# A two-layer attention and MLP kernel: four block sums of a weight matrix made one turn later, and one of two squares made on ScalarE in all five passes

## The chip, the cores and the metric

The kernel runs on one core of a Trainium2 chip. The metric is the device time of one execution in microseconds (us). PE is the matmul engine, DVE is VectorE, ACT is ScalarE, POOL is GpSimd, SP is the queue that issues DMAs.

## The reference

Attention with a window of 128 positions over 4 x 8 heads of 576 positions, then two MLP layers on 2304 tokens of width 512 with a hidden width of 2048. Only the first layer's activation and the second layer's weights are touched by the change.

```python
attn_out = _attn_ref(q, k, v)                     # windowed softmax attention
x = attn_out.transpose(0, 2, 1, 3).reshape(B * S, H * D)     # 2304 x 512
# layer 1
h = x @ w_in                                      # 512 -> 2048
r = np.maximum(h, 0.0)
g = r * r
x = g @ w_out                                     # 2048 -> 512
# layer 2, with its own weights
h = x @ w_in2
y = (h * np.tanh(softplus(h))) @ w_out2
```

## The kernel before

All products are made in a reduced-precision matmul format, so that each operand is split into a high part (a rounded copy) and a low part (the operand less its high part), and three products stand for one.

**Passes and steps.** Layer 1 runs in five passes j = 0 to 4 over blocks of tokens, each with 16 steps fc, one for each 128 columns of the hidden layer. Step "2.8" below is pass 2, step 8. Pass 1 has 256 tokens and the others 512. In one step PE makes the scores of one attention unit of the next block, then `h` of this step (L594, 12 matmuls), at some steps transposes and attention outputs, and then the second product of the step before: `m_out` part 0 with the high part of `g` (L622, L623, 8 matmuls) and part 1 with the low part of `g` (L626, 4 matmuls). Every engine works through its own instructions in the order in which the code writes them.

**The activation of layer 1.** `relu2_a` makes r = relu(h) on ACT, the high part g[:,0] = r squared in the matmul format (ACT, L676), and gg = r squared in full fp32. In passes 0, 1 and 4 gg is made by ACT (L673), ahead of g; in passes 2 and 3 by POOL (L675). `relu2_b` makes the low part g[:,1] = gg - g[:,0] on DVE (L681), in the next step, ahead of that step's softmax. There is one tile r, one tile gg and two tiles g.

**The second layer's weights, prepared in passes 2 to 4.** A turn i (0 to 33) brings in one of 32 pieces of weights: ACT shifts it (`c_lower`, L843), DVE puts its bits together (`c_bits`, L848, L851, L854). Four pieces make a group m; turn 4m + r is its turn r. Pieces 4m and 4m + 1 belong to the first matrix, and the four sums of their blocks, `c_sums` (L866 to L869, tiles s), are made on DVE in passes 2 and 3 and on POOL in pass 4. The second matrix's sums (`c_sums2`, L880 to L884, tiles t) are always on POOL. Each finished tile is then split: ACT writes the high part (`c_split`, L892, tiles c), DVE puts the low part in place over the tile (`c_lows`, L935), and both are stored by DMA at the next step.

**Which steps have a turn.** Passes 2 and 3 have one at steps 2, 3, 4, 6, 7, 8, 10, 11, 12, 14, 15, eleven in each; pass 4 at steps 0 to 11. Turn 0 is at step 2.2, turn 11 at step 3.2, turn 22 at step 4.0. The order on DVE in a step with a turn is: low part of g of the step before (L681), softmax of a unit, bits of the turn's piece, sums if there are any, low parts of the tiles split in this turn. On POOL a step holds the low parts of the attention operands (L262, L264), the sums of the second matrix, gg in passes 2 and 3, and the masks of the probabilities (L473).

Of the kernel before, what the change touches and what calls it, by code (L numbers as in the profile page):

```python
# [13 lines left out]
AF = mybir.ActivationFunctionType  # L14
ALU = mybir.AluOpType
# [18 lines left out]
def two_layers(  # L34
# [16 lines left out]
    nc = tc.nc  # L51
# [91 lines left out]
    NB = len(blocks)  # L143
# [514 lines left out]
    def relu2_r(j, fc):  # L658
        n = size[j]
        ph = hps.pop((0, j, fc))  # L660
        r = gp.tile([P, 512], F32, tag="r", name=f"r{j}_{fc}")
        nc.scalar.activation(r[:, 0:n], ph[:, 0:n], AF.Relu)  # L662
        return r

    def relu2_a(j, fc, r=None):
        n = size[j]
        r = r or relu2_r(j, fc)
        g = gs[0, j, fc] = gp.tile([P, 2, 512], F32R, tag="g", name=f"g0_{j}_{fc}", bufs=2)
        gg = gp.tile([P, 512], F32, tag="gg", name=f"gg{j}_{fc}")
        if j in (0, 1, NB - 1):  # L670


            nc.scalar.activation(gg[:, 0:n], r[:, 0:n], AF.Square)  # L673
        else:
            nc.gpsimd.tensor_tensor(gg[:, 0:n], r[:, 0:n], r[:, 0:n], op=ALU.mult)  # L675
        nc.scalar.activation(g[:, 0, 0:n], r[:, 0:n], AF.Square)  # L676
        return g, gg, n

    def relu2_b(a):
# [149 lines left out]
    late, kept, wraw, wf = [], [], {}, {}  # L829
# [8 lines left out]
    def f_tile(name):  # L838
        return ap["c"].tile([P, DM], I32, tag="f", name=name, bufs=9)

    def c_lower(i):
        f = wf[i] = f_tile(f"wf1_{i}")
        nc.scalar.mul(f.bitcast(F32), wraw[i][:, :, 1].bitcast(F32), LOWERED)  # L843

    def c_bits(i):
        t, f = wraw.pop(i), wf[i]
        low, high = t[:, :, 0], t[:, :, 1]
        nc.vector.tensor_scalar(  # L848
            f, f, 3, 0x3FFFFFF8, op0=ALU.logical_shift_left, op1=ALU.bitwise_and
        )  # L850
        nc.vector.scalar_tensor_tensor(  # L851
            f, high, -0x40000000, f, op0=ALU.bitwise_and, op1=ALU.bitwise_or
        )
        nc.vector.scalar_tensor_tensor(  # L854
            f, low, 29, f, op0=ALU.logical_shift_right, op1=ALU.bitwise_or
        )
        wf[i] = f.bitcast(F32)

    def c_sums(m, eng):

        a, b = wf[4 * m], wf[4 * m + 1]
        x, y = (f_tile(f"s{m}_{k}").bitcast(F32) for k in range(2))
        wf["s", m] = x, y
        tt = eng.tensor_tensor
        s1, s2, s3, s4 = x[:, 0:256], x[:, 256:512], y[:, 0:256], y[:, 256:512]
        tt(s1, b[:, 0:256], b[:, 256:512], op=ALU.add)  # L866
        tt(s2, s1, a[:, 0:256], op=ALU.subtract)
        tt(s3, a[:, 0:256], b[:, 0:256], op=ALU.subtract)
        tt(s4, a[:, 256:512], s2, op=ALU.subtract)  # L869

    def c_sums2(m, half):

        b0, b1 = wf[4 * m + 2], wf[4 * m + 3]
        if half == 0:
            wf["t", m] = [f_tile(f"t{m}_{k}").bitcast(F32) for k in range(2)]
        x, y = wf["t", m]
        tt = nc.gpsimd.tensor_tensor
        t1, t2, t3, t4 = x[:, 0:256], x[:, 256:512], y[:, 0:256], y[:, 256:512]
        if half == 0:
            tt(t1, b0[:, 256:512], b0[:, 0:256], op=ALU.subtract)  # L880
            tt(t3, b1[:, 256:512], b0[:, 256:512], op=ALU.subtract)
        else:
            tt(t2, b1[:, 256:512], t1, op=ALU.subtract)
            tt(t4, t2, b1[:, 0:256], op=ALU.subtract)  # L884
# [4 lines left out]
    def c_split(f, dsts):  # L889
        n = f.shape[-1]  # L890
        hi = ap["c"].tile([P, DM], F32R, tag="c", name=f"c{len(wf)}", bufs=4)[:, 0:n]
        nc.scalar.copy(hi, f)  # L892
        late.append((f, hi, dsts))

    def in_w1d(m, at, n):
        return [w1d[m, :, at + k * n : at + (k + 1) * n] for k in range(2)]

    def in_t2d(m, k, many):
        dsts = [t2d[k : k + many, m, :, z * 256 : z * 256 + 256] for z in range(2)]
        return [d.rearrange("k p c -> p k c") for d in dsts]  # L900
# [11 lines left out]
    def c_tick1():  # L912

        m, r = divmod(made["at"], 4)
        if r == 0 and m:
            c_sums2(m - 1, 1)
            c_split(wf.pop(4 * m - 2)[:, 0:256], in_t2d(m - 1, 4, 1))
            c_split(wf.pop(4 * m - 1), in_t2d(m - 1, 5, 2))
        elif r == 1 and m:
            x, y = wf.pop(("t", m - 1))  # L920
            c_split(x, in_t2d(m - 1, 0, 2))
            c_split(y, in_t2d(m - 1, 2, 2))
        elif r == 2 and 4 * m < NW:
            c_split(wf.pop(4 * m), in_w1d(m, 0, 512))
            c_split(wf.pop(4 * m + 1)[:, 256:512], in_w1d(m, 1024, 256))
        elif r == 3 and 4 * m < NW:
            x, y = wf.pop(("s", m))
            c_split(x, in_w1d(m, 1536, 512))
            c_split(y, in_w1d(m, 2560, 512))
        if made["at"] < NW:  # L930
            c_lower(made["at"])

    def c_lows():
        for f, hi, dsts in late:
            nc.vector.tensor_tensor(f, f, hi.bitcast(F32), op=ALU.subtract)  # L935
            for dst, src in zip(dsts, (hi.bitcast(F32), f)):
                if len(dst.shape) == 3:
                    src = src.rearrange("p (d c) -> p d c", c=256)
                kept.append((dst, src))
        late.clear()  # L940

    def c_tick2(j):
        i = made["at"]
        made["at"] += 1
        m, r = divmod(i, 4)
        if i < NW:
            c_bits(i)
            if r == 1:
                c_sums(m, nc.vector if j < NB - 1 else nc.gpsimd)
            elif r == 3:  # L950
                c_sums2(m, 0)
        c_lows()
# [32 lines left out]
    for j in range(NB - 1):  # L985
        for fc in range(FC):
# [26 lines left out]
            if due:  # L1013
                c_tick1()
# [16 lines left out]
            if due:  # L1031
                c_tick2(j)
            m_h(0, j, fc, ps_h, "h")

            if last:
                for c in range(2):
                    x_split(j + 1, c, xp)
                r = relu2_r(j, fc)
            else:
                pend = relu2_a(j, fc)  # L1040
# [17 lines left out]
            if last:  # L1058
                for c in range(2, KC):
                    x_split(j + 1, c, xp)  # L1060
                pend = relu2_a(j, fc, r)
                for i in sc:
                    u_softmax1(i)
                    u_exp(i)
# [506 lines left out]
    j = NB - 1  # L1571
    for fc in range(FC):
# [6 lines left out]
        if due:  # L1579
            c_tick1()  # L1580
# [7 lines left out]
        if due:  # L1588
            c_tick2(j)
        m_h(0, j, fc, ps_h, "h")  # L1590
        pend = relu2_a(j, fc)
        m_out(*prev, 0)
        m_out(*prev, 1)
# [16 lines left out]
    for g in range(24):  # L1610
        s, m = divmod(g, 8)
# [159 lines left out]
```

## Time and profile before

| | |
|---|---|
| runs before | median 865.5 us of 3 (865.05 to 868.47) |
| the profiled execution | 864.87 us; its span 863.1 us, mean granted clock 0.998 |
| PE busy | 848.4 us, 98% |
| DVE, ACT, POOL busy | 654.1, 506.1 and 306.1 us |
| span by stage | pass 0 from about 37 us, pass 2 from about 200, pass 3 from about 305, pass 4 from about 413, the second layer from about 506 to the end |

The 1.8 us between the span and the execution's own time lie around the span. In a row of a timeline the first number is the start in us from the span's start and the second the busy time in us; "x4" means four instructions in one piece; a bracket at the end gives the idle time of that engine just before, and who ended it. Durations in rows on a tile are in ns.

### The profile page before, as it was taken

The page shows a single profiled execution, that of the slowest core. Times are in us where ns is not written, and L with a number is a line of the kernel's source. Part 1 is how long each engine was busy: PE and PEld are TensorE (multiplying, and loading weights), DVE is VectorE, ACT ScalarE, POOL GpSimd, SP SyncE. Part 2 cuts the span into 40 slices and gives each one's busy share as a digit, 9 for nine tenths or more (in the row PEclk, how much of TensorE's full clock was granted, in tenths as well). Part 3 has the DMA queues.
Part 4 walks back from the last instruction along what each step waited for, and adds up shares of the span by engine and source line. Part 5 has one row for each costly group of instructions (what it writes and reads, how often), then busy time and mean ns, then how long its engine had stood idle before and what let it go on. Part 6 is the DMA issues. An engine that isn't in the chain of part 4 may idle for free.

```text
span 863.1 us, 15492 instructions
## 1 busy us (share of the span) xinstructions
PE 848.4 (98%) x4922; PEld 748.2 (87%) x4922; DVE 654.1 (76%) x1444; ACT 506.1 (59%) x1192; POOL 306.1 (35%) x357
## 2 busy tenths in 40 slices
PE   8999999999998999999999999999999999999998
PEld 5687889998887788778888889999899999999887
DVE  6899998656897989888878635588865688755984
ACT  7888788766565666655666543366433547233731
POOL 5312113755694848665334404400024200144000
PEclk9999999999999999999999999999999999999999
DMA  8466695754696668865689968959889598988574
GB/s 293 123 217 205 205 326 162 252 164 137 215 312 219 193 221 281 288 226 189 220 297 297 347 252 278 326 190 305 289 273 318 190 307 284 312 280 291 183 266 153
DMA packets 114144, 213.30 MB, mean 247 GB/s; under 512 B 14352, under 2 KB 51088, under 8 KB 114064
## 3 DMA queue, kind: packets, MB, share of 16 engines
q1 hardware_dynamic: 114064, 212.32, 74.1%
q8 instruction: 40, 0.66, 0.3%
q14 instruction: 40, 0.33, 0.1%
HBM read 165.09 MB, written 47.19 MB: 246 GB/s over the span
## 4 chain that ended last, share of the span: by engine, by line
PE 88%; DVE 6%; issue 2%; POOL 2%; ACT 1%; DMA 1%; POOLq 0%; DVEq 0%; ACTq 0%
PE p L1197 20%; PE h L594 19%; PE m L1340 16%; PE o L626 7%; PE o L622 6%; PE o L623 6%; PE m L1329 4%; PE o L513 3%; PE pt L430 1%; PE sc L335 1%; PE sc L334 1%; DVE wf L935 1%; DVE wf L851 1%; DVE wf L848 1%; DVE g L681 1%
## 5 line engine op out<-in xcount | busy, mean ns | idle before, releaser
L622 PE MATMUL o<-g,wh 128*128 128x512 f32 (+1 forms) x320 | 118.6, 377 | 0.0
L623 PE MATMUL o<-g,wl 128*128 128x512 f32 (+1 forms) x320 | 115.9, 369 | 0.0
L1620 ACT ACTIVATE a<-c 128x384 f32<-128x384 f32 x96 | 50.5, 526 | 108.4 <-DVE c L1656 55.9
L1234 POOL TENSOR_TENSOR s<-a,a 128x384 f32<-128x384 f32 x21 | 21.2, 1011 | 241.3 <-ACT a L1620 241.3
L1340 PE MATMUL m<-tt,hi 128*128 128x512 f32 x400 | 94.1, 390 | 0.0
L473 POOL TENSOR_SCALAR_AFFINE_SELECT pT<-p 128x128 f32<-128x128 f32 (+2 forms) x80 | 55.8, 719 | 89.4 <-ACT p L461 89.2
L626 PE MATMUL o<-g,wh 128*128 128x512 f32 (+1 forms) x320 | 80.7, 374 | 6.7 <-DVE g L681 6.7
L1340 PEld LDWEIGHTS m<-tt,hi 128*128 128x128 f32 x400 | 74.1, 188 | 14.7
L662 ACT ACTIVATE r<-h 128x512 f32<-128x512 f32 (+1 forms) x80 | 44.2, 552 | 65.0 <-PE h L594 59.7
L594 PE MATMUL h<-xh,wh 128*128 128x512 f32 (+1 forms) x320 | 81.8, 377 | 0.0
L594 PE MATMUL h<-xl,wh 128*128 128x512 f32 (+1 forms) x320 | 79.0, 369 | 0.0
L594 PE MATMUL h<-xh,wl 128*128 128x512 f32 (+1 forms) x320 | 78.9, 368 | 0.0
L681 DVE TENSOR_TENSOR g<-gg,g 128x512 fp32r<-128x512 f32 (+1 forms) x80 | 66.3, 828 | 14.7 <-ACT g L676 8.9
L626 PEld LDWEIGHTS o<-g,wh 128*128 128x128 f32 x320 | 56.6, 190 | 19.1 <-DVE g L681 9.4
L388 ACT ACTIVATE p<-p,st 128x128 f32<-128x128 f32 (+1 forms) x144 | 59.1, 413 | 21.7 <-DVE st L373 21.6
L1278 ACT CAST hi<-a 128x384 fp32r<-128x384 f32 x120 | 56.2, 511 | 25.7 <-PE m L1329 11.1
L1303 DVE TENSOR_TENSOR lo<-a,hi 128x384 fp32r<-128x384 f32 x120 | 61.0, 550 | 10.9 <-PE m L1340 7.9
L622 PEld LDWEIGHTS o<-g,wh 128*128 128x128 f32 x320 | 60.5, 189 | 10.1 <-issue 0.5
L623 PEld LDWEIGHTS o<-g,wl 128*128 128x128 f32 x320 | 60.4, 189 | 9.3
L594 PEld LDWEIGHTS h<-xl,wh 128*128 128x128 f32 x320 | 56.9, 189 | 10.4
L594 PEld LDWEIGHTS h<-xh,wl 128*128 128x128 f32 x320 | 56.7, 189 | 10.4 <-DVE wl L130 0.2
L262 POOL TENSOR_TENSOR ulo<-uraw,uhi 128x256 fp32r<-128x256 f32 (+1 forms) x44 | 42.0, 954 | 56.8 <-ACT uhi L259 31.6
(163 smaller groups left out, 2007.7 us busy)
## 6 DMA issues: line engine op xcount, KB each, us to landing
tt<-t2d SPq DMA_DIRECT2D x168, 256.0 KB, 4.8
wraw<-in_w SPq DMA_DIRECT2D x64, 512.0 KB, 4.4
ra<-w1d SPq DMA_DIRECT2D x24, 512.0 KB, 5.0
rc<-w1d SPq DMA_DIRECT2D x24, 512.0 KB, 4.8
rd<-w1d SPq DMA_DIRECT2D x24, 512.0 KB, 5.3
uraw<-in_qkT SPq DMA_DIRECT2D x24, 320.0 KB, 4.3
uraw<-in_qkT SPq DMA_DIRECT2D x24, 256.0 KB, 4.7
wh<-wsd SPq DMA_DIRECT2D x12, 512.0 KB, 5.7
```

Of the source, the lines that this page charges most:

```text
L388: nc.scalar.activation(probs(i, s), probs(i, s), AF.Exp, bias=u.st[:, s : s + 1], scale=-1.0, accum_out=u.st[:, sums + s : sums + 1 + s],)
L473: nc.gpsimd.affine_select(out=u.pT[:, 0:heads, k : 2 * n : 2, :][:, :, a:], in_=p[:, 0:heads, a:n], pattern=[[0, heads * (n - a)], [0, P / ...
L594: nc.tensor.matmul(ph[:, 0:n], w[:, c * P : (c + 1) * P], xs[j, c][k][:, 0:n], start=t == 0, stop=t == len(terms) - 1,)
L622: nc.tensor.matmul(o, wh[:, ws], g[:, 0, r], start=start, stop=False)
L623: nc.tensor.matmul(o, wl[:, ws], g[:, 0, r], start=False, stop=False)
L626: nc.tensor.matmul(o, wh[:, ws], g[:, 1, r], start=False, stop=stop)
L681: nc.vector.tensor_tensor(g[:, 1, 0:n], gg[:, 0:n], g[:, 0, 0:n].bitcast(F32), op=ALU.subtract)
L1197: nc.tensor.matmul(ps, w[:, z, c * P : (c + 1) * P], t[c], start=n == 0, stop=n == 5)
L1278: nc.scalar.copy(hi, left(s, q))
L1303: nc.vector.tensor_tensor(lo, left(s, q), hi.bitcast(F32), op=ALU.subtract)
L1340: nc.tensor.matmul(o[c][:, r], a, ts2[s, q][:, r], start=start, stop=stop)
L1620: nc.scalar.activation(block(s, BLK[name[1:3]], m), u, AF.Mish)
```

## The change

`c_sums` moves from turn r = 1 to turn r = 2 of its group. There the tiles it reads have been split already, and `c_lows` will overwrite them in the same turn, so the sums are written ahead of `c_lows`; the tiles leave the table `wf` in `c_sums` and no longer in `c_tick1`. In `relu2_a` ACT makes gg in every pass, after g and no longer ahead of it.

```diff
@@ relu2_a
-        if j in (0, 1, NB - 1):
-            nc.scalar.activation(gg[:, 0:n], r[:, 0:n], AF.Square)
-        else:
-            nc.gpsimd.tensor_tensor(gg[:, 0:n], r[:, 0:n], r[:, 0:n], op=ALU.mult)
         nc.scalar.activation(g[:, 0, 0:n], r[:, 0:n], AF.Square)
+        nc.scalar.activation(gg[:, 0:n], r[:, 0:n], AF.Square)
@@ c_sums
-        a, b = wf[4 * m], wf[4 * m + 1]
+        a, b = wf.pop(4 * m), wf.pop(4 * m + 1)
@@ c_tick1
         elif r == 2 and 4 * m < NW:
-            c_split(wf.pop(4 * m), in_w1d(m, 0, 512))
-            c_split(wf.pop(4 * m + 1)[:, 256:512], in_w1d(m, 1024, 256))
+            c_split(wf[4 * m], in_w1d(m, 0, 512))
+            c_split(wf[4 * m + 1][:, 256:512], in_w1d(m, 1024, 256))
@@ c_tick2
             c_bits(i)
-            if r == 1:
+            if r == 2:
                 c_sums(m, nc.vector if j < NB - 1 else nc.gpsimd)
             elif r == 3:
                 c_sums2(m, 0)
         c_lows()
```

By the table of turns the sums were made at steps 2.3, 2.8, 2.14, 3.4, 3.10 and 3.15 on DVE, and at 4.3 and 4.7 on POOL. They are now made at 2.4, 2.10, 2.15, 3.6 and 3.11 on DVE, and at 4.0, 4.4 and 4.8 on POOL: the sixth group goes over from DVE to POOL, since its turn now falls into pass 4.

The first place is DVE at step 2.8, before the change, from the last bits of piece 5 (tile `wf1_5`) to the low part of g of that step (`g0_2_8`, which stands at the start of step 2.9); `s1_0`, `s1_1` are the sums of group 1, `t0_0`, `t0_1` the second matrix's sums of group 0.

```order
L854 SCALAR_TENSOR_TENSOR wf1_5_3482<-wraw1_5_3419,wf1_5_3482 128x512
L866 TENSOR_TENSOR s1_0_3505<-wf1_5_3482 128x256
L867 TENSOR_TENSOR s1_0_3505<-s1_0_3505,wf1_4_3413 128x256
L868 TENSOR_TENSOR s1_1_3506<-wf1_4_3413,wf1_5_3482 128x256
L869 TENSOR_TENSOR s1_1_3506<-wf1_4_3413,s1_0_3505 128x256
L935 TENSOR_TENSOR t0_0_3340<-t0_0_3340,c1_3478 128x512
L935 TENSOR_TENSOR t0_1_3341<-t0_1_3341,c1_3480 128x512
L681 TENSOR_TENSOR g0_2_8_3528<-gg2_8_3529,g0_2_8_3528 128x512
```

After the change the four sums are gone from this place: the bits are followed at once by the two low parts of t and the low part of g.

The second place is DVE at step 2.10 of the change, from the last bits of piece 6 to the low part of g of that step. Lines are five less than before from here on in the code (L849 was L854, L930 was L935, L676 was L681).

```order
L849 SCALAR_TENSOR_TENSOR wf1_6_3613<-wraw1_6_3488,wf1_6_3613 128x512
L861 TENSOR_TENSOR s1_0_3626<-wf1_5_3482 128x256
L862 TENSOR_TENSOR s1_0_3626<-s1_0_3626,wf1_4_3413 128x256
L863 TENSOR_TENSOR s1_1_3627<-wf1_4_3413,wf1_5_3482 128x256
L864 TENSOR_TENSOR s1_1_3627<-wf1_4_3413,s1_0_3626 128x256
L930 TENSOR_TENSOR wf1_4_3413<-wf1_4_3413,c2_3609 128x512
L930 TENSOR_TENSOR wf1_5_3482<-wf1_5_3482,c2_3611 128x256
L676 TENSOR_TENSOR g0_2_10_3649<-gg2_10_3650,g0_2_10_3649 128x512
```

Before, the same place held the bits, the two low parts and the low part of g, without the four sums.

The third place is ACT at steps 2.8 and 2.9 of the change: the cast of an attention operand (`uhi`), two high parts, the shift of piece 5, then r, g, gg and the exponentials of a unit, and the cast of step 2.9.

```order
L259 CAST uhi60_3473<-uraw60_3400 128x512
L887 CAST c1_3478<-t0_0_3340 128x512
L887 CAST c1_3480<-t0_1_3341 128x512
L838 ACTIVATE wf1_5_3482<-wraw1_5_3419 128x512
L662 ACTIVATE r2_8_3520<-h0_2_8_3507 128x512
L670 ACTIVATE g0_2_8_3522<-r2_8_3520 128x512
L671 ACTIVATE gg2_8_3523<-r2_8_3520 128x512
L388 ACTIVATE p58_3494,st58_3495<-p58_3494,st58_3495 128x128 x2
L259 CAST uhi61_3547<-uraw61_3471 128x512
```

Before, the exponentials followed g directly, and gg stood on POOL, behind what POOL had ahead of it, as here for steps 2.7 and 2.8.

```order
L883 TENSOR_TENSOR t0_0_3340<-wf1_3_3324,t0_0_3340 128x256
L884 TENSOR_TENSOR t0_1_3341<-t0_0_3340,wf1_3_3324 128x256
L675 TENSOR_TENSOR gg2_7_3447<-r2_7_3444 128x512
L473 AFFINE_SELECT pT55_3377<-p54_3201 128x4x128 x2
L262 TENSOR_TENSOR ulo60_3474<-uraw60_3400,uhi60_3473 128x256
L264 TENSOR_TENSOR uhi60_3473<-uraw60_3400,uhi60_3473 64x256
L675 TENSOR_TENSOR gg2_8_3529<-r2_8_3526 128x512
```

In the change the two rows of gg are gone from POOL; its other rows keep their order.

## Rows read from the trace of the kernel before

**Rows 1.** Page, part 1: busy time by engine, share of the span, instructions.

```profile
PE 848.4 (98%) x4922; PEld 748.2 (87%) x4922; DVE 654.1 (76%) x1444; ACT 506.1 (59%) x1192; POOL 306.1 (35%) x357
```

**Rows 2.** Waits of PE, whole span: engine, line, releaser: us in total, times, longest.

```profile
PE o L626 <- DVE g L681: 6.7, 4, 2.5
PE pt L427 <- POOL p L417: 2.4, 6, 0.8
```

**Rows 3.** Timeline of the matmul engine around its four stalls, passes 2 and 3.

```profile
start us, us, engine line op out<-in xcount [idle before <-releaser]
...
262.72 1.21 PE L626 MATMUL o<-g,wh 128*128 128x512 f32 x4 [2.50 <-DVE g L681]
...
284.88 1.07 PE L626 MATMUL o<-g,wh 128*128 128x512 f32 x4
...
286.26 1.09 PE L594 MATMUL h<-xh,wh 128*128 128x512 f32 x4
...
291.99 1.19 PE L626 MATMUL o<-g,wh 128*128 128x512 f32 x4 [1.01 <-DVE g L681]
...
347.15 2.08 PE L626 MATMUL o<-g,wh 128*128 128x512 f32 x4 [2.21 <-DVE g L681]
...
349.88 1.30 PE L594 MATMUL h<-xh,wh 128*128 128x512 f32 x4
...
374.49 1.19 PE L626 MATMUL o<-g,wh 128*128 128x512 f32 x4 [1.01 <-DVE g L681]
```

**Rows 4.** Stretch at stall three: length, busy PE, PEld, DVE, ACT, POOL, granted clock, DMA.

```profile
344.90:348.30 3.40, 1.19 (x4) 0.96 (x4) 3.05 (x10) 0.50 (x3) 1.03 (x1) 0.79 0.44 146
```

**Rows 5.** Instructions on tile gg (min/median/max ns), and one wait (us, times).

```profile
L681 DVE TENSOR_TENSOR g<-gg,g x80: 407/684/1511, 45.0 to 505.1; 128x512 fp32r<-128x512 f32 x64, 128x256 fp32r<-128x256 f32 x16
L673 ACT ACTIVATE gg<-r x48: 416/632/637, 40.6 to 503.9; 128x512 f32<-128x512 f32 x32, 128x256 f32<-128x256 f32 x16
L675 POOL TENSOR_TENSOR gg<-r x32: 1039/1320/1583, 206.2 to 413.8; 128x512 f32<-128x512 f32 x32
...
  POOL gg L675: 5.6, 6
```

**Rows 6.** Timeline of VectorE, steps 2.7 to 2.9.

```profile
244.78 0.88 DVE L681 TENSOR_TENSOR g<-gg,g 128x512 fp32r<-128x512 f32 x1 [0.94 <-POOL gg L675]
...
249.69 2.40 DVE L935 TENSOR_TENSOR wf<-wf,c 128x256 f32<-128x256 f32 x2
...
255.72 1.26 DVE L848 TENSOR_SCALAR wf<-wf 128x512 int32<-128x512 int32 x1
...
259.31 0.42 DVE L866 TENSOR_TENSOR s<-wf 128x256 f32<-128x256 f32 x1
...
260.78 1.28 DVE L935 TENSOR_TENSOR t<-t,c 128x512 f32<-128x512 f32 x2
```

**Rows 7.** Timeline of VectorE, steps 2.10 to 2.12.

```profile
267.49 0.42 DVE L848 TENSOR_SCALAR wf<-wf 128x512 int32<-128x512 int32 x1
...
270.00 1.01 DVE L935 TENSOR_TENSOR wf<-wf,c 128x512 f32<-128x512 f32 x2
270.94 0.68 DVE L681 TENSOR_TENSOR g<-gg,g 128x512 fp32r<-128x512 f32 x1
274.67 0.30 DVE L294 COPY_PREDICATED sc<-bias_sb,sc 128x128 f32<-128x128 int16 x1 [3.05 <-PE sc L335]
...
282.08 1.14 DVE L681 TENSOR_TENSOR g<-gg,g 128x512 fp32r<-128x512 f32 x1 [0.93 <-POOL gg L675]
```

**Rows 8.** Timeline of ScalarE, step 2.7.

```profile
243.84 0.73 ACT L259 CAST uhi<-uraw 128x640 fp32r<-128x640 f32 x1 [1.02 <-PE sc L335]
```

**Rows 9.** Timeline of GpSimd, steps 4.7 and 4.8: a set of sums.

```profile
460.12 1.12 POOL L866 TENSOR_TENSOR s<-wf 128x256 f32<-128x256 f32 x1 [5.88 <-DVE wf L854]
...
463.50 0.73 POOL L869 TENSOR_TENSOR s<-wf,s 128x256 f32<-128x256 f32 x1
```

**Rows 10.** Timeline of VectorE, step 4.8: the low parts behind those sums.

```profile
465.89 1.57 DVE L935 TENSOR_TENSOR wf<-wf,c 128x512 f32<-128x512 f32 x2
```

## The prediction

> **What bounds the kernel now.** I read the page first: PE is busy for 848.4 of 863.1 us, the others for 654 us at most [rows 1]. So the kernel is bound by PE, and an edit that takes no work from PE can win only what PE waits. The view of waits names it all: 6.7 us in four pieces before L626, each released by L681 on DVE, and 2.4 us in the opening attention, which the change doesn't reach [rows 2]. The four are the place to look.
>
> On PE's timeline they stand at the starts of steps 2.9 and 2.13 and, with the same durations to a few tenths, 3.5 and 3.9: 2.50, 1.01, 2.21 and 1.01 us of idle [rows 3]. PE has done part 0 of the second product and lacks the low part of g. Behind each wait PE also runs slower for a moment: four L626 take 1.21, 1.19 and 1.19 us, where an unstalled set takes 1.07 [rows 3]. After the third wait it is worse. From L626 to the next h takes 349.88 - 347.15 = 2.73 us against 286.26 - 284.88 = 1.38, and that h 1.30 against 1.09 [rows 3]. In this stretch the granted clock falls to a mean of 0.79, part of it at 1.2 GHz in place of 2.4, after PE had waited 2.2 us [rows 4]. The 2.5 us wait at 2.9 shows no such drop, so I don't count on one for each wait.
>
> What the four cost PE: idle 2.50 + 1.01 + 2.21 + 1.01 = 6.73; slow restarts 0.14 + 0.12 + 0.12 for the three light ones and 1.35 + 0.21 = 1.56 for the third, 1.94 together. **8.7 us is the ceiling of the change.**
>
> Why is L681 late? On DVE, steps 2.6 to 2.8 run nearly without a gap, and what stretches them is of three kinds. L681 waits 0.94 us for POOL's gg at 2.7 [rows 6]. The same waits stand at 2.12 (0.93, [rows 7]) and at four more places, 5.6 us in six [rows 5]. The four sums stand in 2.8, from 259.31 to 260.78, 1.47 us [rows 6]. And instructions are slow while POOL works: the low parts of 256 + 512 columns take 2.40 us at 249.69, L848 takes 1.26 us at 255.72 [rows 6], where at 2.10 they take 1.01 and 0.42 [rows 7].
>
> **The square.** 32 instructions of 1.04 us at least (median 1.32) leave POOL, and ACT gets as many of about 0.63, the cost of its own ones in passes 0, 1 and 4 [rows 5]. ACT is busy for 506 of 863 us [rows 1]. gg stands behind r and g and ahead of the exponentials, so what ACT does after it shifts by up to 0.63 us. What hides this is the wait of ACT's next cast for PE's scores, 1.02 us at the head of step 2.7 [rows 8]; then the high parts, the shift and DVE's bits start when they did. Without that cover DVE's bits would come 0.63 us later in each of 22 turns. I take nothing. ACT's gg must also wait for L681 of the step before, since there is one tile gg. But the exponentials behind it wait for a softmax that DVE does after that L681 anyway, so nothing new is queued. In passes 0, 1 and 4 g and gg swap; L681 needs both, so nothing.
>
> What DVE wins: the waits for gg, 0.94 us ahead of each of the four stalls. ACT has gg done some 1.3 us after r starts, while DVE is still at its bits. To this comes the slowing under POOL. The 1.39 us by which the 2.40 exceeds 1.01 lay under gg and under one of POOL's sums; the 0.84 us of L848 lay under gg, but the next POOL instruction will move up into its place. I take 0.7 us a run, bounds 0 and 1.39 + 0.84 = 2.2.
>
> The skill has a rule here. The Trainium skill, "SBUF — State Buffer", section "Who interferes with whom", says that a VectorE instruction with two SBUF inputs and a GpSimd instruction that reads SBUF share a read port, and that the later one blocks fully until the first is done. The slowed instructions agree in kind. By it a removed square could give DVE all its 1.04 us, 3.1 us in a run of three in place of my 0.7; the stalls would go all the more and PE's sum stays, only my main case would be surer, 0.75 in place of 0.66.
>
> **The sums.** At 2.8 and 3.4, each right ahead of a big stall, DVE loses 1.47 us of work. With the 0.94 and 0.7 that is 3.1 us (bounds 2.4 and 4.6) against waits of 2.50 and 2.21: both go, with the lower bound falling short by 0.1. At 2.13 and 3.9 no sums go, 0.94 + 0.7 = 1.6 us (bounds 0.94 and 3.1) against 1.01: both go, short by 0.1 each at the lower bound.
>
> Then the places where the sums arrive. At 2.10 L681 ends at 271.62, and DVE then idles 3.05 us until scores that PE makes behind the L626 in question [rows 7]. These L626 and scores take about 1.5 us, so the low part is some 1.5 us early now. The sums cost 1.47 us if POOL is quiet. But DVE also comes to this step earlier against PE, by the 0.6 us that 3.1 exceeds 2.5, and the gg that lay on the bits there is gone. I take no wait; with sums stretched by the 1.26/0.42 of L848 to 4.4 us, it would be 2.3 us. At 2.4, 2.15, 3.6 and 3.11 the same holds with a gap or a step without a turn near, and I take nothing. ACT splits the sums one step after they are made at 2.11, 3.7 and 3.12, and there its order is cast of scores, then split, so it comes to them when DVE is through.
>
> In pass 4 the sums are on POOL. They took from 460.12 to 464.23 there, 4.1 us, starting as soon as the bits of turn r = 1 were done [rows 9]; written a turn later, they still wait for nothing else but their tile. New is that DVE's low parts must wait until POOL has read the two tiles. In step 4.8 those start at 465.89 [rows 10], 1.7 us after POOL's end: nothing. The sixth group's sums leave DVE for POOL at 4.0.
>
> **The sum.** 6.73 + 1.94 = 8.7 us off the profiled 864.87 gives 856.2. The median of the runs is 0.6 above that execution: 856.8. I leave 0.2 us for a remnant: **857.0 us**. This measurement can tell about 0.5%, 4.3 us, from no change.
>
> **The rivals.**
> - *The stalls move* (0.13). The sums at 2.10, 3.6 or 3.11 fall under POOL's work and PE waits there, up to 2.3 us each, perhaps with one slow restart of 1.56: 857 + 2.3 + 1.56 = 861. For it: 0.42 becomes 1.26 in the same code [rows 6, 7]. Against it: 3.05 us of idle on DVE.
> - *The waits re-form* (0.13). DVE gets no relief from POOL, since POOL's other work closes up, and loses its lead in the turns behind; then the two waits of 1.01 us and half of the big ones stay, or all: 861 to 866, say 864.
> - *ACT becomes the late engine* (0.05, the other side). The place is ACT's cast at the head of a step. If its idle of 1.02 us is less than the 0.63 of the added square in most steps, the 32 squares come to lie on the chain ACT, bits, L681, PE: 32 x 0.63 = 20 us, less the 5.6 us of waits for gg that end: up to 865.5 + 14.6 = 880. It decides when ACT's mean spare time in a step falls under 0.6 us. Against it: 1.02 us where the step is tight [rows 8].
> - *POOL holds DVE in pass 4* (0.03). The set of sums starts late because its tile isn't yet stored, and the low parts wait in 4.0, 4.4 and 4.8. At most 3 x 4.1 = 12.3 us come back, with the 8.7 won: 869. It needs a start over 1.7 us later than now [rows 9, 10]. By the skill's port rule, above, POOL's reads would also block DVE's other instructions there; no row separates the two.
>
> **Chances and range.** Main case 0.66, at 856 to 858. Faster by over 0.5% (under 861.2): 0.66, 0.09 from the moved stalls and 0.02 from the re-formed: 0.77. Within 0.5%: 0.04 + 0.11 = 0.15. Slower: the last two rivals, 0.08. The range goes from 855.3, all four stalls won at the pace of the quickest run, 865.05 - 8.7 less a margin of 1 us, to 862.0, which takes in the moved stalls and leaves 0.2 out.
>
> **What would show it.** In the changed profile PE's waits before L626 should be gone or under 1 us in all, passes 2 and 3 together about 8 us shorter, and the granted clock 1.0 through 3.5. L681 should show no wait of 0.9 us behind gg; POOL should lose 42 us (32 x 1.32) and ACT gain 20. The low part of g should come at 2.10 and 3.11 ahead of PE, though with less to spare, and DVE's low parts in pass 4 should not wait for POOL. I am wrong if waits before L626 stand at new steps (the sums), if casts on ACT start without idle and bits wait for ACT (the square), or if the L626 waits are gone and the time is not: then PE's busy time has grown, and the ceiling was misread.

## The result, and the profile after

The changed kernel takes 856.74 us (median of 4 runs, 855.76 to 857.98) beside 865.86 for the one before (4 runs): a ratio of 0.989 with a 95% interval of 0.9864 to 0.9916, so 8.4 to 13.6 in 1000 less. Its profiled execution took 855.76 us, with a span of 854.0.

The page's first part, busy time by engine:

```profile
PE 845.2 (99%) x4922; PEld 747.0 (87%) x4922; DVE 635.7 (74%) x1440; ACT 523.3 (61%) x1224; POOL 269.1 (32%) x329
```

Beside [rows 1], POOL lost 37.0 us and ACT gained 17.2; PE's 4922 matmuls are the same. What no edit asked for is that DVE, with four instructions fewer (sums that went to POOL in pass 4), is busy for 18.4 us less.

The waits of PE (us in total, times, longest), where [rows 2] had 6.7 us before L626:

```profile
PE pt L427 <- POOL p L417: 3.2, 7, 1.2
PE idle L686 <- POOL ident masks.py:199: 1.4, 1, 1.4
```

There is no row for L626 any more. On PE's timeline, the four places that stalled in [rows 3], steps 2.9, 2.13, 3.5 and 3.9, stand without idle and at nearly the unstalled pace:

```profile
260.08 1.07 PE L626 MATMUL o<-g,wh 128*128 128x512 f32 x4
...
288.02 1.07 PE L626 MATMUL o<-g,wh 128*128 128x512 f32 x4
...
340.65 1.07 PE L626 MATMUL o<-g,wh 128*128 128x512 f32 x4
...
365.24 1.16 PE L626 MATMUL o<-g,wh 128*128 128x512 f32 x4
```

Executions differ by up to 1.7 us in their opening, ahead of pass 2, so kernels are compared below from the L626 that takes the g of step 2.0 to the one that takes that of step 4.0, "passes 2 and 3" or "between the marks". Of this stretch the view by windows gives start and end, length, busy time of PE, PEld, DVE, ACT and POOL, granted clock, DMA share and GB/s; first before, then after:

```profile
210.85:428.68 217.83, 211.10 (x1105) 174.23 (x1104) 188.22 (x369) 133.15 (x312) 134.62 (x137) 0.99 0.73 237
```

```profile
210.88:419.38 208.50, 208.50 (x1106) 173.25 (x1105) 170.39 (x365) 148.81 (x343) 100.45 (x110) 1.00 0.76 247
```

The stretch is 9.33 us shorter, as much as the whole span lost (863.1 to 854.0, 9.1), and PE is busy in all of it. DVE does nearly the same work, four sums less (some 2.4 us at their mean of 0.6 before), in 17.8 us less, though none of its other instructions was edited. That is the lead that the experiments follow.

VectorE's timeline of steps 2.7 to 2.10, to be laid beside [rows 6, 7] (start, us, line, idle before):

```profile
248.71 2.03 DVE L930 TENSOR_TENSOR wf<-wf,c 128x256 f32<-128x256 f32 x2
250.67 1.16 DVE L676 TENSOR_TENSOR g<-gg,g 128x512 fp32r<-128x512 f32 x1
...
254.13 0.42 DVE L843 TENSOR_SCALAR wf<-wf 128x512 int32<-128x512 int32 x1
...
255.91 1.85 DVE L930 TENSOR_TENSOR t<-t,c 128x512 f32<-128x512 f32 x2
257.69 1.23 DVE L676 TENSOR_TENSOR g<-gg,g 128x512 fp32r<-128x512 f32 x1
...
266.17 0.42 DVE L861 TENSOR_TENSOR s<-wf 128x256 f32<-128x256 f32 x1
...
268.70 0.68 DVE L676 TENSOR_TENSOR g<-gg,g 128x512 fp32r<-128x512 f32 x1
```

The L848 of 1.26 us ahead of the first stall is the L843 of 0.42 now; the sums stand in 2.10; the low part of g there ends at 269.38, and PE asks for it at 270.23, 0.85 us later.

### The profile page after: what moved, and what is told of

Its sections match the earlier page's. It is cut to its first block, busy times and chain, and to the rows that moved or that the text cites. A ratio compares the mean times of both kernels' runs of the same rounds, so it can differ in the third digit from the quotient of the medians.

```text
span 854.0 us, 15409 instructions
## 1 busy us (share of the span) xinstructions
PE 845.2 (99%) x4922; PEld 747.0 (87%) x4922; DVE 635.7 (74%) x1440; ACT 523.3 (61%) x1224; POOL 269.1 (32%) x329
## 4 chain that ended last, share of the span: by engine, by line
PE 97%; DVE 1%; ACT 1%; POOL 0%; issue 0%; POOLq 0%; DVEq 0%
PE h L594 23%; PE p L1192 20%; PE m L1335 16%; PE o L622 8%; PE o L626 8%; PE o L623 8%; PE m L1324 4%; PE o L513 3%; PE pt L430 2%; PE sc L335 1%; PE sc L334 1%; ACT p L388 1%; PE sc L338 1%; PE pt L427 0%; DVE p L373 0%; PE o L553 0%
## 5 line engine op out<-in xcount | busy, mean ns | idle before, releaser
L473 POOL TENSOR_SCALAR_AFFINE_SELECT pT<-p 128x128 f32<-128x128 f32 (+2 forms) x80 | 54.0, 696 | 106.0 <-ACT p L461 105.6
L626 PE MATMUL o<-g,wh 128*128 128x512 f32 (+1 forms) x320 | 79.5, 370 | 0.0
L676 DVE TENSOR_TENSOR g<-gg,g 128x512 fp32r<-128x512 f32 (+1 forms) x80 | 63.4, 793 | 10.1 <-ACT gg L671 10.1
L626 PEld LDWEIGHTS o<-g,wh 128*128 128x128 f32 x320 | 56.3, 189 | 11.2 <-DVE g L676 1.4
```

The lines of the kernel that those rows point to most:

```text
L473: nc.gpsimd.affine_select(out=u.pT[:, 0:heads, k : 2 * n : 2, :][:, :, a:], in_=p[:, 0:heads, a:n], pattern=[[0, heads * (n - a)], [0, P / ...
L626: nc.tensor.matmul(o, wh[:, ws], g[:, 1, r], start=False, stop=stop)
L676: nc.vector.tensor_tensor(g[:, 1, 0:n], gg[:, 0:n], g[:, 0, 0:n].bitcast(F32), op=ALU.subtract)
```

## The experiments

Two explanations compete for the 9.3 us. *Stretching*: POOL's instructions lengthen those of DVE that run beside them. *Lateness*: DVE waits for what POOL makes late (gg), or POOL's queue is late for other reasons. Beside them stand the sums, and the rivals of the prediction.

The length and DVE's busy time are those of passes 2 and 3, PE's waits those of the whole span; the kernel before took 866.23 us (median of 19 runs) beside the first four kernels and 866.36 (17 runs) beside the others.

| kernel | median us (runs) | ratio to the kernel before, 95% interval | passes 2 and 3, us | PE's waits before L626: us, times | DVE busy, us |
|---|---|---|---|---|---|
| before | 865.86 (4) | | 217.83 | 6.7, 4 | 188.22 |
| after | 856.74 (4) | 0.9864 to 0.9916 | 208.50 | none | 170.39 |
| sums alone | 865.04 (12) | 0.9975 to 1.0003 | 215.74 | 5.1, 5 | 188.25 |
| square alone | 858.08 (4) | 0.9886 to 0.9917 | 209.60 | 0.6, 2 | 170.27 |
| 64 half squares on POOL | 862.91 (6) | 0.9942 to 0.9976 | 214.37 | 4.1, 3 | 188.54 |
| ACT's square twice | 857.28 (4) | 0.9877 to 0.9908 | 209.21 | 0.5, 1 | 175.85 |
| 32 squares on POOL | 867.02 (10) | 0.9991 to 1.0016 | 216.63 | 5.2, 6 | 190.91 |
| the same of another tile | 869.14 (8) | 1.0015 to 1.0046 | 221.18 | 7.7, 6 | 192.93 |
| 128 memsets on POOL | 857.44 (4) | 0.9884 to 0.9914 | 208.40 | none | 170.07 |
| order of g and gg as before | 857.3 (1) | | 208.48 | none | 171.75 |

**1. The sums alone.** The changed kernel, with the squares of passes 2 and 3 on POOL as before:

```
-        nc.scalar.activation(gg[:, 0:n], r[:, 0:n], AF.Square)
+        if j in (0, 1, NB - 1):
+            nc.scalar.activation(gg[:, 0:n], r[:, 0:n], AF.Square)
+        else:
+            nc.gpsimd.tensor_tensor(gg[:, 0:n], r[:, 0:n], r[:, 0:n], op=ALU.mult)
```

> The four sums a turn later, the square as before (POOL makes gg in passes 2 and 3). My theory (both parts are needed, each takes its own share of the lateness): the sums free 1.47 us ahead of the stalls at 2.9 and 3.5, so waits of about 1.0 and 0.7 us stay there without the slow restart of 1.56; the waits at 2.13 and 3.9 stay at 1.0 each or grow, since 3.6 now holds sums; with POOL's gg on the bits a wait of up to 1.5 us may come at 2.10. Waits before L626 3.5 to 6 us in all, time 860 to 863. Rival (the sums alone do it, the square is without effect): no waits, about 857. Rival (the square alone does it): as before the change, 865 to 866.

Measured: 865.04 us, where 860 to 863 was expected; the interval of the ratio holds 1, so no gain is shown by the times. Its PE timeline at the steps in question:

```profile
261.93 1.19 PE L626 MATMUL o<-g,wh 128*128 128x512 f32 x4 [0.61 <-DVE g L681]
...
291.18 1.20 PE L626 MATMUL o<-g,wh 128*128 128x512 f32 x4 [1.01 <-DVE g L681]
...
344.76 1.20 PE L626 MATMUL o<-g,wh 128*128 128x512 f32 x4 [0.63 <-DVE g L681]
...
372.81 1.19 PE L626 MATMUL o<-g,wh 128*128 128x512 f32 x4 [2.45 <-DVE g L681]
...
401.43 1.20 PE L626 MATMUL o<-g,wh 128*128 128x512 f32 x4 [0.38 <-DVE g L681]
```

The two big stalls of [rows 3] fall from 2.50 and 2.21 to 0.61 and 0.63, by 1.89 and 1.58 us, somewhat more than the 1.47 us that the sums take [rows 6]. But 3.9 goes from 1.01 to 2.45, and a fifth wait appears at 3.13. The sums that left 3.4 stand in 3.6 now, where POOL still works beside them, and the 1.44 us more at 3.9 are about their length; yet run 5 below has them there too and waits 0.74 at 3.9, so this cause is argued and not shown. The waits moved, and in the profiled executions 2.1 us of passes 2 and 3 was won.

**2. The square alone.** The kernel before with the change of the square; the sums stay at r == 1:

```
-        if j in (0, 1, NB - 1):
-            nc.scalar.activation(gg[:, 0:n], r[:, 0:n], AF.Square)
-        else:
-            nc.gpsimd.tensor_tensor(gg[:, 0:n], r[:, 0:n], r[:, 0:n], op=ALU.mult)
         nc.scalar.activation(g[:, 0, 0:n], r[:, 0:n], AF.Square)
+        nc.scalar.activation(gg[:, 0:n], r[:, 0:n], AF.Square)
```

> ACT makes gg in all passes, g first; the sums stay at turn r = 1. My theory: 0.94 us of wait for gg and up to 0.7 us of slowing go, 1.6 us in each of the four runs: the waits at 2.13 and 3.9 go, those at 2.9 and 3.5 stay with about 0.9 and 0.6 us. Waits before L626 about 1.5 us in all, time 858 to 859.5. If POOL's other work closes up and only the 0.94 goes: 1.6 and 1.3 us at the big stalls, 0 to 0.1 at the small ones, time 859 to 861. Rival (the square is without effect): 865 to 866. Rival (it does all): 857.

Measured: 858.08 us. The waits of its PE:

```profile
PE o L626 <- DVE g L676: 0.6, 2, 0.3
```

The stalls at 2.13 and 3.9 are gone; those at 2.9 and 3.5, where the sums still stand, are 0.28 and 0.32 us. So the square alone gives 8.2 of the 9.3 us, and the sums on top of it 1.1. Without the square the sums gave 2.1 us in the one profile and nothing clear of noise in the times, so by far the most is the square's.

**3. Work put back on POOL, in half squares.** POOL squares both halves of r into an unused tile in passes 2 and 3; nothing waits for the result:

```
+        if j in (2, 3):
+            z = ap["w"].tile([P, 1, 2, P], F32, tag="pT", name=f"z{j}_{fc}", bufs=1)
+            z = z.rearrange("p o b c -> p (o b c)")
+            for k in range(2):
+                rk = r[:, k * 256 : (k + 1) * 256]
+                nc.gpsimd.tensor_tensor(z, rk, rk, op=ALU.mult)
```

> The changed kernel, but POOL still works for as long as it did: at the place of gg it makes two squares of 256 columns of r into a tile that nobody reads (results unused), 1.5 to 2 us a step in passes 2 and 3. ACT makes the gg that counts. This splits the square's gain into the wait for gg (stays away) and POOL's load on DVE (comes back). If the wait was all of it: L626 waits 0 to 0.3 us, 857. If the load counted with the 0.7 us a run that I took: the low part of g, which is early by 1.16, 0.55, 1.17 and 0.08 us at 2.9, 2.13, 3.5 and 3.9 in the changed kernel, is late by 0.2 at 2.13 and 0.6 to 0.7 at 3.9: waits of 0.5 to 1.5 us, 857.5 to 858.5. By the full block of the port rule (up to 1.04 us a square, three in a run): waits of 2 to 3 us in each of the four places, 865 or more.

Measured: 862.91 us, 5.9 of the 9.3 us between the marks lost again, with waits of 1.27, 1.32 and 1.52 us at 2.9, 3.5 and 3.9; the time lies between its second forecast and its third. No gg comes from POOL here, so the waits don't need it. But POOL got more work than it had lost, 64 instructions of 0.94 us against 32 of 1.32, and the kernel is yet not as slow as before; and ACT's r waited 13.5 us, four times, for POOL to have read it. This run doesn't settle it.

**4. ACT's square twice.** One more of ACT's squares for each gg of passes 2 and 3:

```
-        nc.scalar.activation(gg[:, 0:n], r[:, 0:n], AF.Square)
+        for _ in range(2 if j in (2, 3) else 1):
+            nc.scalar.activation(gg[:, 0:n], r[:, 0:n], AF.Square)
```

> The changed kernel with gg made twice over on ACT in passes 2 and 3 (same tile, same values): the suspected cost of the square doubled, 0.54 us more on ACT in each of 32 steps. My theory (ACT's wait for scores hides it; 1.02 us at 2.7 before, some 0.5 left): mostly hidden, but the last of the cover goes at tight steps: waits before L626 0 to 1 us, chiefly at 3.9 where the low part is 0.08 us early, time 857 to 858.5. Rival (ACT is on the chain already): 32 x 0.54 = 17 us more, 870 or above.

Measured: 857.28 us. ACT's busy time between the marks rises by 18.0 us and the stretch by 0.7, one wait of 0.52 us at 3.9, the step where the changed kernel had 0.08 us to spare. ACT's cover bears twice what the change laid on it. DVE is busy for 175.85 us here, 5.5 more than after the change, though POOL's instructions are the same: a difference of this size is no sign of more load on POOL, and the ones read below are three to four times as large.

**5. Exactly the old load on POOL.** As 3, but one instruction of 512 columns, the one that was removed, into an unused tile:

```
+            nc.gpsimd.tensor_tensor(z.bitcast(BF16), r, r, op=ALU.mult)
```

> The changed kernel, with one square of 512 columns of r on POOL at the place where gg was (result unused, into a spare 16-bit tile), 1.3 us a step: the load that the change took away, and no more; nobody waits for it but the next r, as before. Theory after the first four runs: POOL's load on DVE is most of the square's gain, not the wait for gg. Then passes 2 and 3, 208.5 us in the changed kernel and 214.4 with the heavier load, take 212 to 214 us, the waits before L626 come to 2.5 to 4 us, and the time is 860.5 to 862.5. Rival (the first look's 5.9 us came from the excess of its load, 1.7 against 1.3 us a step): 209 to 210 us, 857 to 858.

Measured: 867.02 us, the time before, and more than either forecast. Waits of PE, and VectorE's timeline in step 2.8, the place of the rows at 254.13 and 255.91 above:

```profile
PE o L626 <- DVE g L680: 5.2, 6, 1.7
```

```profile
256.65 1.26 DVE L847 TENSOR_SCALAR wf<-wf 128x512 int32<-128x512 int32 x1
257.95 1.11 DVE L850 SCALAR_TENSOR_TENSOR wf<-wraw,wf 128x512 int32<-128x512 int32 x1
259.09 1.11 DVE L853 SCALAR_TENSOR_TENSOR wf<-wraw,wf 128x512 int32<-128x512 int32 x1
260.13 2.13 DVE L934 TENSOR_TENSOR t<-t,c 128x512 f32<-128x512 f32 x2
262.18 0.68 DVE L680 TENSOR_TENSOR g<-gg,g 128x512 fp32r<-128x512 f32 x1
```

gg is made by ACT, DVE waits for no gg of POOL's, and the gain is gone: of passes 2 and 3 8.1 of 9.3 us, of the whole time all. Run 1 is its pair: the sums stand at the same place, POOL makes the gg that counts, and DVE waits for it, 6.5 us in seven pieces between the marks. Here DVE waits for none of it, and passes 2 and 3 take 216.63 us against 215.74. Some 1.6 us of this is a drop of the granted clock at 3.5, a mean of 0.69 from 346.50 to 350.00 us, which run 1 doesn't have (8.52 us from that L626 to the next, 6.95 in run 1). So by this pair, with POOL's reads in place, the end of the wait for gg is worth some 0.7 us at most. From the bits to the end of the low part of g it takes 262.86 - 256.65 = 6.2 us here, and 258.92 - 254.13 = 4.8 in the changed kernel. POOL's timeline beside it:

```profile
256.26 1.37 POOL L675 TENSOR_TENSOR z<-r 128x512 bf16<-128x512 f32 x1
257.60 0.92 POOL L262 TENSOR_TENSOR ulo<-uraw,uhi 128x256 fp32r<-128x256 f32 x1
258.59 1.07 POOL L264 TENSOR_TENSOR uhi<-uraw,uhi 64x256 fp32r<-64x256 f32 x1
260.28 1.43 POOL L675 TENSOR_TENSOR z<-r 128x512 bf16<-128x512 f32 x1 [0.62 <-ACT r L662]
```

The square takes 1.37 us of POOL, its other work moves behind it and then lies beside DVE's bits. What this run leaves to the other side: one wait of ACT's r for POOL's read (4.4 us), and two short waits of DVE for POOL's t, 0.63 us some steps ahead of 2.9 and 0.64 ahead of 3.5. The first:

```profile
251.52 1.51 DVE L934 TENSOR_TENSOR wf<-wf,c 128x512 f32<-128x512 f32 x1 [0.63 <-POOL t L883]
```

**6. The same load, of another tile.** As 5, but POOL squares a tile xh, so that r is free of it:

```
+            x = xs[j, 0][0].bitcast(F32)
+            nc.gpsimd.tensor_tensor(z.bitcast(BF16), x, x, op=ALU.mult)
```

> As pool_same, but the idle square reads a tile that was there long before (the high part of the block's input), so that neither POOL waits for r nor ACT's next r for POOL. It has the same length and reads as much. If DVE is slowed by POOL's reads: passes 2 and 3 take 211 to 214 us, time 859.5 to 862.5, much as pool_same. If the tie between r and POOL was what cost: 208.5 to 209.5 us, 857.

Measured: 869.14 us, slower than before and outside both forecasts. The edit brought a wait of its own, at the two block boundaries, where ACT writes the next xh (waits of ACT):

```profile
ACT xh L571 <- POOL z L676: 6.8, 2, 3.9
```

The first of these stands at 309.69 us. Neither reaches PE: from the L626 of the g of 2.13 to that of 3.3 it takes 39.97 us, beside 39.90 before and in run 5, and from that of 3.12 to that of 4.0 26.24, as in run 5. What costs is PE's waits before L626, 2.16, 0.77, 1.74 and 2.61 us at the old four places, and the granted clock behind the first and the last (0.64 from 264.40 to 268.00 us, 0.75 from 375.00 to 381.00). The waits at 2.9 and 2.13 stand ahead of the boundary, with r never held: 2.50 and 1.01 were there in [rows 3], 1.68 and 0.74 in run 5. So the hold on r isn't the cause. Why 3.9 has 2.61 here and 0.74 in run 5 stays open.

**7. As busy, without reading.** In place of the square, four memsets of the unused tile, which read nothing:

```
+            for _ in range(4):
+                nc.gpsimd.memset(z, 0.0)
```

> As pool_free, but POOL is kept busy by four memsets of 256 columns (1.2 us a step by its memsets of 128 columns, 0.2 us each), which read nothing. POOL's later instructions stand in its queue as long as in pool_free. If DVE is slowed by POOL's reads (the shared read port): its instructions run at full pace under the memsets, passes 2 and 3 take 208.5 to 210 us, time 857 to 858. Rival (POOL's own lateness costs: masks and low parts of the attention come later, whatever the filling is): as pool_free, 211 to 214 us, 860 to 862.

Measured: 857.44 us, no wait before L626. The window of passes 2 and 3:

```profile
212.07:420.47 208.40, 208.40 (x1105) 173.32 (x1104) 170.07 (x365) 148.68 (x343) 133.52 (x233) 1.00 0.76 247
```

POOL is as busy as before the change (133.52 us, before 134.62; in run 5 141.42). On its timeline at step 2.8 the memsets take 1.59 us where the square of run 5 took 1.37, and the two instructions behind them end as late as there, 259.60 against 259.66 us:

```profile
255.57 1.59 POOL L676 MEMSET z<- 128x256 f32 x4
257.62 0.83 POOL L262 TENSOR_TENSOR ulo<-uraw,uhi 128x256 fp32r<-128x256 f32 x1 [0.46 <-ACT uhi L259]
258.53 1.07 POOL L264 TENSOR_TENSOR uhi<-uraw,uhi 64x256 fp32r<-64x256 f32 x1
```

VectorE's timeline beside it, to be laid beside that of run 5:

```profile
254.83 0.96 DVE L848 TENSOR_SCALAR wf<-wf 128x512 int32<-128x512 int32 x1
255.83 0.69 DVE L851 SCALAR_TENSOR_TENSOR wf<-wraw,wf 128x512 int32<-128x512 int32 x1
256.56 0.69 DVE L854 SCALAR_TENSOR_TENSOR wf<-wraw,wf 128x512 int32<-128x512 int32 x1
257.17 1.83 DVE L935 TENSOR_TENSOR t<-t,c 128x512 f32<-128x512 f32 x2
258.92 1.22 DVE L681 TENSOR_TENSOR g<-gg,g 128x512 fp32r<-128x512 f32 x1
```

And the last of the bits over all of passes 2 and 3, in run 5 and here (busy us, mean ns):

```profile
L853 DVE SCALAR_TENSOR_TENSOR wf<-wraw,wf 128x512 int32<-128x512 int32 x24 | 24.8, 1033 | 0.8
```

```profile
L854 DVE SCALAR_TENSOR_TENSOR wf<-wraw,wf 128x512 int32<-128x512 int32 x24 | 18.3, 763 | 0.8
```

DVE is busy for 170.07 us, as in the changed kernel, where the squares of run 5 made it 190.91. POOL's added instructions of 7 stand at the same place, last as long and write more than those of 5, but they read nothing; between the two lie 20.8 us of DVE's busy time and 8.2 us of passes 2 and 3 (1.6 of it the clock at 3.5 in run 5). *Stretching* stands, and *lateness* falls as the main cause. A remnant of it can't be ruled out: the two waits for t of run 5, 0.63 and 0.64 us, are in run 6 too and not here.

**8. The order of g and gg.** ACT makes gg first, as passes 0, 1 and 4 had it:

```
+        nc.scalar.activation(gg[:, 0:n], r[:, 0:n], AF.Square)
         nc.scalar.activation(g[:, 0, 0:n], r[:, 0:n], AF.Square)
-        nc.scalar.activation(gg[:, 0:n], r[:, 0:n], AF.Square)
```

> The changed kernel with gg ahead of g on ACT in all passes. The low part of g needs both, and the high part is wanted a step later: no change in passes 2 and 3 (208.5 us within 0.5), time within 1 us of the changed kernel. Rival (g must come first since the high part holds up PE): waits before L622 in the view of PE's waits, some 0.5 us a step.

Measured: 208.48 us between the marks, one run of 857.3. The swap does nothing, as the prediction had it.

## Why the prediction was right, point by point

It said 857.0 us, and 856.74 came. The reading of the bound holds: PE was busy nearly throughout, the four waits were all there was to win, and they went.

- **The ceiling, 8.7 us.** The stretch won 9.33, the span 9.1. By the two windows, PE's idle of 217.83 - 211.10 = 6.73 us is gone, as taken, and PE's busy time, with the slow restarts and the dip of the clock at 3.5 [rows 4] in it, falls by 211.10 - 208.50 = 2.60, where 1.94 was taken. The mechanism was right, the term of the slow restarts 0.7 too small, and the 0.2 left for a remnant wasn't needed.
- **The square: right in sign, wrong in its parts.** "The waits for gg, 0.94 us ahead of each of the four stalls" were counted as DVE's gain, and "the slowing under POOL" as 0.7 us a run, bounds 0 to 2.2. By runs 1 and 5, the end of the wait for gg is worth some 0.7 us of passes 2 and 3 at most as long as POOL reads as much as before: DVE spends the time won on slower instructions instead. By run 2, with the squares gone from POOL, the stalls shrink by 2.50 - 0.28 = 2.22 and 2.21 - 0.32 = 1.89 us. Most of this is then the slowing, near its upper bound of 2.2; what the wait would be worth without the slowing, no run shows. That 1.6 us forecast stands so near to 1.9 to 2.2 measured is luck: one part was too large and the other too small.
- **The rule of the Trainium skill that was weighed.** The Trainium skill, "SBUF — State Buffer", section "Who interferes with whom", gives reads of two inputs by VectorE and reads by GpSimd one port. Runs 5 and 7 agree with it: squares that read cost DVE 20.8 us, memsets that read nothing cost it none in sum. By it the prediction had 3.1 us a run of slowing, 4.0 with the 0.94 of the wait; 1.9 to 2.2 in all were measured at PE, nearer to the 1.6 forecast, while the share that is slowing lies well above the 0.7 taken. Whether each of the 32 squares blocks DVE fully isn't shown: 20.8 us are about half of the 32 x 1.37 = 44 us that they take (1.37 is their median in run 5), and not each has a DVE instruction of two inputs beside it all the time. "The slowed instructions agree in kind" goes too far: L848, which went from 0.42 to 1.26 us [rows 6, 7], has one input in its row, so the rule on two inputs doesn't reach it.
- **The sums: 1.47 us about right, but hardly needed.** Run 1 shows 1.89 and 1.58 us less at the two stalls; beside the square, what the sums had left to end was 0.28 and 0.32 us of wait, 1.1 us of passes 2 and 3. Run 1 also shows the rival of the moved stalls, at 3.9 with 2.45 us and at 3.13 with 0.38. In the changed kernel, with the squares gone from POOL, 3.9 is met with 0.08 us to spare and 2.10 with 0.85, where the prediction saw "some 1.5". "I take no wait" came true, at 3.9 only just. The prediction saw for 2.10 that the gg on the bits would be gone, but gave that rival a chance that doesn't hang on the square.
- **ACT: right.** Its casts still start after idle (0.57 us ahead of that at 243.91, where [rows 8] had 1.02), and run 4 speaks against the late engine at twice the load: 0.7 us, where that rival had 17.
- **Pass 4: right.** POOL's sums of 4.1 us stand there again, and the one wait of DVE for POOL (2.42 us, ahead of an L930 at 470.57) stood there before with 2.41. From the L626 of 4.0 on, over the next 90.62 us, PE is busy without a gap before and after. That rival wasn't tried further.
- **What would show it.** No waits before L626, passes 2 and 3 about 8 us shorter, the clock at 1.0, POOL down by about 42 and ACT up by 20: the first three came, POOL's 42 as 37.0, less some 4 for the set of sums that went to it, and ACT's 20 as 17.2.

Open: why 64 half squares (60 us of POOL) cost PE less than 32 whole ones (run 3 against run 5; 1.6 of the 2.3 us between them is the clock at 3.5 in run 5), and how much of the slowing is full blocking and how much a slower pace.

## What to carry to other kernels

When VectorE feeds the bound engine, ask whether GpSimd reads SBUF beside it. In this kernel that had a price which no view of waits showed: it lay in VectorE's busy time, so compare the duration of the same instruction with GpSimd busy and idle. Such work can be cheaper on ScalarE as long as that has idle ahead of its next due instruction: here 32 squares of 0.63 us cost nothing measurable there, and some 8 us of the whole on GpSimd. A wait of 0.94 us on the late engine that is removed need not be a gain: as long as what stretches that engine stays, it can be spent again.

## What the runs showed that was not expected

- Memsets on POOL leave VectorE's busy time in sum as it was, but not each instruction. The first of the bits, of one input (TENSOR_SCALAR, L843 after, L848 with the memsets), takes 721 ns in the mean from 210 to 430 us there and 596 in the changed kernel; the last, of two inputs (SCALAR_TENSOR_TENSOR, L849 and L854), takes 760 there and 771 in the changed kernel.
- The length of PE's wait alone doesn't tell whether the clock falls after it. The granted clock fell after the 2.21 us at 3.5 before (mean 0.79, [rows 4]) and in run 5 already after 1.71 us (0.69). But no drop shows after the 2.50 us at 2.9 before, nor in run 1, whose 2.45 us at 3.9 are followed by an L626 of 1.19 us in place of 2.08, and whose granted clock is 1.00 over passes 2 and 3.
